# The end of the first token block: two chunks of the second product and their copies placed ahead of the second block, routing constants given a fixed place

## The chip, the core and the metric

The kernel runs as one program on one core of a Trainium2 chip. The core has five engines that each work through their own queue in order: TensorE (PE, the matmuls; PEld is its weight load), ScalarE (ACT), VectorE (DVE), GpSimd (POOL) and SyncE (SP, which here only issues DMAs). An instruction that waits for a semaphore holds up what stands behind it on its own engine. The metric is the device time of one execution in microseconds (us); lower is better.

## The reference, cut to what matters

Three stages follow one another: an attention with a band of 16 positions and 24 block summaries for each of 2 batches and 8 heads, a feed-forward layer, and a routed layer of 8 experts of which each token takes one.

```python
x = attention(q, k, v)                       # 1536 tokens x 512
h = x @ w_in                                 # 512 -> 2048
g = np.where(h > 0.0, h, np.exp(np.minimum(h, 0.0)) - 1.0)
x = g @ w_out                                # 2048 -> 512
logits = x @ w_gate
e_idx = np.argmax(logits, axis=1)            # one expert for each token
gate_w = softmax(logits)[e_idx]
eom = 1.0 / (1.0 + np.exp(-(x @ w_output_gate)))
for e in range(8):
    out[mask_e] = gate_w * eom * (np.maximum(x[mask_e] @ w1[e], 0.0) @ w2[e])
```

## The kernel before, in words

**Tiling.** The 1536 tokens are cut into 24 units of 64 queries, and these into four blocks of 8, 4, 6 and 6 units (512, 256, 384 and 384 tokens). For each block the feed-forward layer runs over 16 chunks of 128 of the 2048 hidden columns. A chunk c of block j is made of these steps: `mm_h` (line 482: 12 matmuls, hidden values h from x and the chunk of w_in, each operand in a high and a low part), `elu` (lines 495, 502 and 508: two on ACT, two on DVE, the result elp), `g_high` and `g_low` (lines 518 on ACT and 524 on DVE: high and low part of elp), `w_high` and `w_low` (lines 175 on ACT and 179 on DVE: the same of the chunk of w_out, wsp), and `mm_y` (line 543: three matmuls for each 128 tokens, added up over the chunks in the PSUM banks y). Block 0 has four y tiles, block 1 two. After chunk 15 `out_y1` copies each y tile out (line 557 on ACT; tile 1 on DVE, line 555) and stores it to DRAM by a DMA on SP's queue (line 564).

**Banks.** The y banks are four, so block 0 fills them all, and block 1's first `mm_y` needs two of them copied out. The banks for h are two, so `mm_h` of a chunk needs line 508 of the chunk two before it to be through.

**What sets the order.** Block 0 together with the attention of its own units, the conversion of the weights and the attention of block 1 is written out by hand in the string `START`, one token for an instruction group; `start_up` plays it, and all engines keep that order up to where later work is moved in. In it Yc stands for `mm_y` of chunk c, fc, gc for `g_low` and `g_high`, ic, jc for `w_high` and `w_low`, oa and ob for the attention products of units 10 and 11, ha and la for `x_hi` and `x_lo` of that pair (lines 455 and 462: the high and low part of block 1's last x), F4 for a reduction of v (line 239). After it `part1` runs steps i = 16 to 63: `mm_h` of step i, the splits, `elu`, then `mm_y` of step i - 2. So Y of chunks 14 and 15 of block 0 lies in `part1`, behind the first and the second `mm_h` of block 1, and the copies of y behind that. There only PE's order is by hand; the other engines' order is the result of a simulated schedule, which may move an instruction ahead into the stretch of `START`.

**Mid-block work.** `vsums2` brings sums of v from DVE's result to a tile pad by four DMAs on SP (line 246), and three `v_pad` on DVE (line 255) read it. Scores of the attention units 12 and 13 (line 330 on PE, line 340 on DVE, line 353 on ACT) come in step 17. `route_consts` loads 404 columns of constants by one DMA (rc) and prepares the routing tiles from them on POOL (lines 771 to 789, twelve instructions); the routing needs them once the first logits of block 0 are made. It is written at the start of block 1, and the simulated schedule moves it to the kernel's beginning, since it waits for nothing.

Of the kernel before, what the change touches and what calls it, by code (L numbers as in the profile page):

```python
# [13 lines left out]
U32 = mybir.dt.uint32  # L14
# [8 lines left out]
E, F2 = 8, 1024  # L23
# [14 lines left out]
NF = FF // 128  # L38
# [43 lines left out]
class Prog:  # L82
# [533 lines left out]
    def part1(self):  # L616
        nc = self.nc
        self.NKV = 3
        self.gate = {}
        self.prev = None  # L620
        self.rw, self.ev, self.cond = {}, {}, {}
        self.ew, self.xg, self.xs, self.g2, self.gT = {}, {}, {}, {}, {}
        self.raw, self.cvf, self.w, self.u, self.x, self.g, self.y, self.m, self.h, self.st, self.wsp = ({} for _ in range(11))
        self.ks = [self.const.tile([128, NP, NB], F32, name=f"ks{b}") for b in range(B)]
        self.v = [self.const.tile([128, 512], F32, name=f"v{i}") for i in range(self.NKV)]
        self.fv, self.mT, self.mt, self.hl, self.y2, self.o2, self.tx, self.par = {}, {}, {}, {}, {}, {}, {}, {0: 0, 1: 1}
        self.kT, self.cv, self.te, self.nmean, self.vs = {}, {}, {}, 0, None
# [12 lines left out]
        todo = {}  # L640

        def at(hs, fn, *args):
            todo.setdefault(hs, []).append((fn, args))

        for j in range(2, NBLK):
            for n in range(UNITS[j]):
                u = U0[j] + n
                h0 = PAIRS[u - n % 2]
                if UPB <= u < UPB + self.NKV:
                    at(h0 + 7, self.v_pad, u)  # L650
                at(max(2 * NF, h0 - LQ), self.load_q, u)
# [24 lines left out]

        h0 = 2 * NF * (NBLK - 1)
        at(h0 + ER, self.route_early)
        at(h0 + EI, self.early_lists)
        for n in range(2):  # L680
            at(h0 + ER + 2, self.w_expert, n)
            at(h0 + EI, self.x_load, n)
        at(h0 + XT, self.x_all, 0)
        at(h0 + XT + 3, self.x_all, 1)
        for i in range(16):
            at(h0 + max(2 * i + 1, ER + 2), self.w_load, 0, i)
            if i < WN:
                at(h0 + max(2 * i + 6, WC + i // 2), self.w_conv, 0, i)
                at(h0 + max(2 * i + 6, WC + i // 2), self.w_load, 1, i)

        def run(hs):
            for fn, args in sorted(todo.pop(hs, []), key=lambda x: rank.get(x[0].__name__, 5)):
                name = fn.__name__
                n = URGENT.get(name, 0) if hs >= 2 * NF * (NBLK - 1) else 0
                with self.tc.high_priority(offset=n) if n else ExitStack():
                    fn(*args)

        with self.tc.manual_schedule(engines={mybir.EngineType.PE}):
            for i in range(NF, len(steps)):
# [867 lines left out]
```

## Time and profile before

| | |
|---|---|
| median of 3 runs | 527.0 us (526.36 to 528.31) |
| profiled execution, its own time | 526.98 us |
| its span (first to last instruction) | 525.2 us |
| PE busy | 511.6 us, 97% of the span |
| DVE busy | 337.1 us, 64% |
| ACT busy | 305.1 us, 58% |
| POOL busy | 54.4 us, 10% |
| DMA | 78.08 MB, mean 149 GB/s |

The page's busy shares are means over the span. Matmuls are pipelined and their ends are modelled, so PE's pace is read from where one group starts to where the next starts, and its waits from the idle time in square brackets and the engine that ended it. "Granted clock" is the share of full speed that TensorE was given.

### The profile page before, as it was taken

How to read it: one execution, taken by the hardware profiler on the slowest of the kernel's cores; microseconds unless marked ns; L12 is line 12 of the kernel's file. 1: busy time of each engine (PE TensorE's matmuls, PEld its weight loads, DVE VectorE, ACT ScalarE, POOL GpSimd, SP SyncE). 2: the span in 40 equal slices, each digit the busy share in tenths (PEclk: the TensorE clock that was granted, in tenths of full speed). 3: DMA queues.
4: the chain of work that ended last, by engine and by line, in shares of the span. 5: the costliest groups of instructions: out<-in, count | busy, mean ns of one | idle time of the engine just before them, and what ended most of it. 6: DMA issues, size and time to landing. Idle time of an engine off the chain costs nothing. (4 is left out here: it accounts for less than half of the span.)

```text
span 525.2 us, 9833 instructions
## 1 busy us (share of the span) xinstructions
PE 511.6 (97%) x3325; PEld 409.6 (78%) x3325; DVE 337.1 (64%) x945; ACT 305.1 (58%) x715; POOL 54.4 (10%) x102
## 2 busy tenths in 40 slices
PE   9999999998999999999999999999999999999994
PEld 6486778886888889888898897987888567576883
DVE  5899999997688868676557899668321011535410
ACT  3899998994677658656546547543232223656421
POOL 3530000001000000000000000113411111100001
PEclk9999999999999999999999999999999999999998
DMA  8999334551311212200001025310689898594601
GB/s 293 405 396 331 119 118 140 179 195 50 132 32 52 81 45 78 82 0 16 2 0 62 1 75 192 96 61 1 183 319 302 297 360 317 174 344 149 203 22 43
DMA packets 37131, 78.08 MB, mean 149 GB/s; under 512 B 3951, under 2 KB 9807, under 8 KB 37072
## 3 DMA queue, kind: packets, MB, share of 16 engines
q1 hardware_dynamic: 34752, 70.02, 39.2%
q0 software_dynamic: 2320, 7.34, 4.0%
q8 instruction: 28, 0.46, 0.4%
q14 instruction: 31, 0.25, 0.2%
HBM read 100.37 MB, written 6.55 MB: 204 GB/s over the span
## 5 line engine op out<-in xcount | busy, mean ns | idle before, releaser
L482 PE MATMUL h<-xh,wi 128*128 128x384 f32 (+2 forms) x528 | 142.8, 338 | 2.5 <-DVE elp L508 1.5
L543 PE MATMUL y<-wsp,gh 128*128 128x512 f32 x368 | 117.3, 400 | 0.0
L482 PEld LDWEIGHTS h<-xh,wi 128*128 128x128 f32 x528 | 94.5, 190 | 10.7 <-DVE elp L508 2.4
L482 PE MATMUL h<-xl,wi 128*128 128x384 f32 (+2 forms) x264 | 87.9, 333 | 1.6 <-DVE xl L462 1.6
L543 PEld LDWEIGHTS y<-wsp,gh 128*128 128x128 f32 x368 | 66.8, 190 | 12.3 <-issue 0.5
L543 PE MATMUL y<-wsp,gl 128*128 128x512 f32 x184 | 72.5, 394 | 0.0
L1222 DVE TENSOR_TENSOR holdl<-S,holdh 128x512 fp32r<-128x512 f32 x22 | 15.2, 690 | 72.5 <-ACT holdh L1218 53.7
L1190 PE MATMUL h<-w2s,holdh 128*128 128x512 f32 x176 | 59.8, 400 | 0.0
L1233 PE MATMUL y<-w2s,holdh 128*128 128x512 f32 x176 | 59.0, 398 | 0.0
L482 PEld LDWEIGHTS h<-xl,wi 128*128 128x128 f32 x264 | 50.2, 190 | 5.6 <-DVE xl L462 1.8
L502 DVE SCALAR_TENSOR_TENSOR elt<-ele,elt 128x384 f32<-128x384 f32 (+2 forms) x64 | 35.5, 554 | 24.6 <-ACT ele L495 24.3
L495 ACT ACTIVATE elt<-h 128x384 f32<-128x384 f32 (+2 forms) x64 | 31.2, 487 | 31.1 <-PE h L482 30.5
L175 ACT CAST wsp<-wo 128x512 fp32r<-128x512 f32 x62 | 38.0, 617 | 16.8 <-PE y L543 16.0
L179 DVE TENSOR_TENSOR wsp<-wo,wsp 128x512 fp32r<-128x512 f32 x62 | 42.6, 689 | 6.3 <-ACT wsp L175 6.0
L518 ACT CAST gh<-elp 128x384 fp32r<-128x384 f32 (+2 forms) x62 | 31.5, 508 | 23.5 <-DVE elp L508 12.8
L524 DVE TENSOR_TENSOR gl<-elp,gh 128x384 fp32r<-128x384 f32 (+2 forms) x62 | 34.0, 549 | 12.2 <-ACT gh L518 11.9
L543 PEld LDWEIGHTS y<-wsp,gl 128*128 128x128 f32 x184 | 34.7, 188 | 8.0 <-DVE gl L524 0.3
L353 ACT ACTIVATE e<-e,nb 128x120 f32<-128x120 f32 x88 | 33.6, 385 | 10.8 <-DVE nb L340 10.8
L1233 PEld LDWEIGHTS y<-w2s,holdh 128*128 128x128 f32 x176 | 33.1, 188 | 8.4 <-issue 1.6
L1190 PEld LDWEIGHTS h<-w2s,holdh 128*128 128x128 f32 x176 | 33.1, 188 | 8.2 <-ACT w2s L1258 0.8
L1264 DVE TENSOR_TENSOR w2s<-wo,w2s 128x512 fp32r<-128x512 f32 x48 | 30.8, 687 | 9.3 <-ACT w2s L1258 7.8
L508 DVE SCALAR_TENSOR_TENSOR elp<-elt,h 128x384 f32<-128x384 f32 (+2 forms) x64 | 35.1, 548 | 0.9
(290 smaller groups left out, 819.8 us busy)
## 6 DMA issues: line engine op xcount, KB each, us to landing
wo<-in_w SPq DMA_DIRECT2D x9, 2048.0 KB
wo<-in_w SPq DMA_DIRECT2D x18, 1024.0 KB
ri<-in_w_in SPq DMA_DIRECT2D x16, 512.0 KB
ro<-in_w_out SPq DMA_DIRECT2D x16, 512.0 KB
wo<-in_w SPq DMA_DIRECT2D x32, 256.0 KB
w2p<-in_w SPq DMA_DIRECT2D x32, 256.0 KB
w2q<-in_w SPq DMA_DIRECT2D x24, 256.0 KB
k<-in_kw SPq DMA_DIRECT2D x18, 192.0 KB
```

The source lines that it names most:

```text
L175: self.nc.scalar.copy(w[:, 0], self.w[c, 1].bitcast(F32))
L179: self.nc.vector.tensor_tensor(w[:, 1], self.w[c, 1].bitcast(F32), w[:, 0].bitcast(F32), op=ALU.subtract)
L353: nc.scalar.activation(e[:, p], e[:, p], AF.Exp, bias=nb[:, p:p + 1], scale=-1.0, accum_out=sm[:, p:p + 1])
L482: nc.tensor.matmul(h, lhsT=w[:, wl, k * 128:k * 128 + 128], rhs=x[:, k, a:b], start=(n == 0), stop=(n == 11))
L495: self.nc.scalar.activation(self.te[j, c][i], self.h[j, c], AF.Exp if i else AF.Tanh, scale=1.0 if i else 0.5)
L502: nc.vector.scalar_tensor_tensor(t, e, 1.0, t, op0=ALU.add, op1=ALU.mult)
L508: nc.vector.scalar_tensor_tensor(p, t, 0.0, h, op0=ALU.min, op1=ALU.max)
L518: self.nc.scalar.copy(gh, p)
L524: self.nc.vector.tensor_tensor(gl, p, gh.bitcast(F32), op=ALU.subtract)
L543: nc.tensor.matmul(self.y[j][t], lhsT=gx[:, sl], rhs=wx, start=(c == 0 and n == 0), stop=(c == NF - 1 and n == len(ops) - 1))
L1190: nc.tensor.matmul(self.h[s, hf], lhsT=x[:, k], rhs=w, start=(n == 0), stop=(n == 11))
L1233: nc.tensor.matmul(self.y2[s], lhsT=g[:, ks], rhs=w, start=(i == 0 and n == 0), stop=(i == 7 and n == 2))
```

## The change

Three edits. In `START`, `X` (the routing constants) stands between `g4` and `Y3`; `Ye` and `Yf` (Y of chunks 14 and 15 of block 0) are put near the end, the second behind `ff`; and `O0` to `O3` (copy of a y tile and its store) close it. `part1` no longer plans the routing constants, and makes `mm_y` of step i - 2 only from step 18 on.

```diff
-START = "... i5 U51 C70 g4 Y3 D7 R8 ... Vf2 fe je jf gf ha F4 ff la"
+START = "... i5 U51 C70 g4 X Y3 D7 R8 ... Vf2 fe je jf gf ha Ye F4 ff Yf la O0 O1 O2 O3"
@@ part1
-        at(2 * NF, self.route_consts)
@@ part1, loop over i from NF
                 self.elu(j, c)
                 run(2 * i + 1)
-                jj, cc = steps[i - 2]
-                self.mm_y(jj, cc)
-                if cc == NF - 1:
-                    self.out_y(jj)
+                if i >= NF + 2:
+                    jj, cc = steps[i - 2]
+                    self.mm_y(jj, cc)
+                    if cc == NF - 1:
+                        self.out_y(jj)
@@ start_up
+                elif k == "X":
+                    self.route_consts()
+                elif k == "O":
+                    self.out_y1(0, *n)
```

PE at the end of block 0, before. Line 449 is the attention product ob, line 482 the first `mm_h` of block 1 (xh1, xl1: its x); Y of chunk 14 follows behind its 12 matmuls:

```order
L449 MATMUL S_1676<-et_1685,v2_100 64x64 [waits DMAHW3_49,Activation_49]
L449 MATMUL S_1676<-et_1685,v2_100 64x64 x7
L482 MATMUL h_1775<-xh1_167,wi0_545 128x256 [waits Activation_49]
L482 MATMUL h_1775<-xl1_168,wi0_545 128x256 [waits DVE_49]
L482 MATMUL h_1775<-xh1_167,wi0_545 128x256 x2
```

PE after. Behind ob stand the 12 matmuls of chunk 14 (line 543, not shown), then chunk 15 (wsp_1685, gh_1748, gl_1764), then block 1:

```order
L543 MATMUL y_822<-wsp_1685,gh_1748 128x512 [waits Activation_49]
L543 MATMUL y_822<-wsp_1685,gh_1748 128x512 [waits DVE_49]
L482 MATMUL h_1811<-xh1_167,wi0_545 128x256 [waits Activation_49]
L543 MATMUL y_822<-wsp_1685,gl_1764 128x512 [waits DVE_49]
L543 MATMUL y_823<-wsp_1685,gh_1748 128x512 x2
L543 MATMUL y_823<-wsp_1685,gl_1764 128x512
L543 MATMUL y_824<-wsp_1685,gh_1748 128x512 x2
L543 MATMUL y_824<-wsp_1685,gl_1764 128x512
L543 MATMUL y_825<-wsp_1685,gh_1748 128x512 x2
L543 MATMUL y_825<-wsp_1685,gl_1764 128x512
L482 MATMUL h_1811<-xl1_168,wi0_545 128x256 [waits DVE_49]
L482 MATMUL h_1811<-xh1_167,wi0_545 128x256 x2
```

The 24 matmuls of chunks 14 and 15 moved ahead of block 1's first `mm_h`; one matmul of that `mm_h`, which needs only xh1, came to stand inside chunk 15. Behind it the two `mm_h`, the scores and the third `mm_h` of block 1 now follow without a Y between them.

ACT behind ha (line 455), before: the two ACT steps of block 1's first `elu` (h_1775) come next, and the first copy of y stands eight rows further on:

```order
L455 CAST xh1_167<-S_1676 128x4x128 [waits PE_49]
L495 ACTIVATE elt_1791<-h_1775 128x256 [waits PE_49]
L495 ACTIVATE ele_1792<-h_1775 128x256 [waits Activation_49]
L518 CAST gh_1826<-elp_1796 128x256 [waits DVE_49,PE_49,Activation_49]
L175 CAST wsp_1913<-wo_101 128x512 [waits PE_49,Activation_49]
L495 ACTIVATE elt_1830<-h_1810 128x256 [waits PE_49]
```

ACT after:

```order
L455 CAST xh1_167<-S_1703 128x4x128 [waits PE_49]
L175 CAST wsp_1913<-wo_101 128x512 [waits DVE_49,PE_49]
L557 ACTIVATE m_1779<-y_822 128x512 [waits PE_49]
L557 ACTIVATE m_1785<-y_824 128x512 [waits PE_49]
L557 ACTIVATE m_1788<-y_825 128x512 [waits PE_49]
L175 CAST wsp_1967<-wo_101 128x512 [waits DVE_49]
L495 ACTIVATE elt_1827<-h_1811 128x256 [waits PE_49]
L495 ACTIVATE ele_1828<-h_1811 128x256
```

Three copies of y and two splits of w_out moved ahead of that first `elu`. On DVE the fourth copy and two splits (line 179) join the three `v_pad` that stood ahead of it already. On SP the four stores moved ahead of the loads of two attention units (k and q); the four pad DMAs keep their place ahead of both.

POOL in the start-up, before (rr and e: sums and exponentials of the attention of units 3, 4 and 6; cv_t: a weight chunk):

```order
L385 TENSOR_SCALAR rr_387<-sm_344 128x4 [waits Activation_49]
L771 CAST wg3_1743<-rc_1741 128x4x16 [waits DMAHW2_49]
L777 CAST tri_1750<-rc_1741 128x128
L783 COPY val_1757<-rc_1741 128x12
L784 COPY val_1757<-rc_1741 128x12
L774 TENSOR_TENSOR r_wg0_1745<-rc_1741,wg3_1743 128x64 [waits Pool_49]
L771 CAST wg3_1743<-r_wg0_1745 128x4x16 [waits Pool_49]
L385 TENSOR_SCALAR rr_429<-sm_398 128x4 [waits DVE_49]
L385 TENSOR_SCALAR rr_467<-sm_391 128x4
L774 TENSOR_TENSOR r_wg0_1745<-r_wg0_1745,wg3_1743 128x64 [waits Pool_49]
L771 CAST wg3_1743<-r_wg0_1745 128x4x16 [waits Pool_49]
L401 TENSOR_TENSOR e_350<-e_350,rr_429 128x480 [waits DVE_49,Activation_49]
```

POOL after, the same place:

```order
L385 TENSOR_SCALAR rr_387<-sm_344 128x4 [waits Activation_49]
L385 TENSOR_SCALAR rr_429<-sm_398 128x4 [waits DVE_49]
L385 TENSOR_SCALAR rr_467<-sm_391 128x4
L401 TENSOR_TENSOR e_350<-e_350,rr_429 128x480 [waits DVE_49,Activation_49]
L156 TENSOR_TENSOR cv_t_393<-cv_t_393,cv_r_394 128x512 [waits Activation_49]
```

The eight constant instructions left this stretch (and four memsets the kernel's very beginning); all twelve now stand on POOL behind its fourth copy of ks, and their DMA stands on SP behind the tenth chunk load of w_out, some 57 us into the span of before.

## Rows read from the trace of the kernel before

**Rows 1.** The page's part 1: busy us, share of span, instructions
```profile
PE 511.6 (97%) x3325; PEld 409.6 (78%) x3325; DVE 337.1 (64%) x945; ACT 305.1 (58%) x715; POOL 54.4 (10%) x102
```

**Rows 2.** Waits of PE: who, line, waited for, us, times, longest
```profile
PE h L482 <- DVE xl L462: 1.6, 1, 1.6
```

**Rows 3.** Stretches: length, busy PE PEld DVE ACT POOL, granted clock, DMA share, GB/s
```profile
42.00:125.00 83.00, 83.00 (x423) 64.81 (x421) 80.90 (x179) 75.84 (x156) 1.32 (x2) 1.00 0.52 167
126.00:129.00 3.00, 0.53 (x2) 0.33 (x3) 2.80 (x5) 0.81 (x2) 0.00 (x0) 1.00 0.25 74
129.00:133.00 4.00, 4.00 (x17) 3.62 (x18) 1.93 (x5) 0.66 (x2) 0.00 (x0) 0.57 0.02 6
```

**Rows 4.** Timeline of PE at the block's end: start, us, what, [idle before <- releaser]
```profile
125.30 0.69 PE L449 MATMUL S<-et,v 120*64 120x64 f32 x16
...
126.86 0.38 PE L482 MATMUL h<-xh,wi 128*128 128x256 f32 x1 [0.87 <-ACT xh L455]
128.85 0.39 PE L482 MATMUL h<-xl,wi 128*128 128x256 f32 x1 [1.61 <-DVE xl L462]
...
131.08 1.05 PE L543 MATMUL y<-wsp,gh 128*128 128x512 f32 x2
...
134.56 0.28 PE L482 MATMUL h<-xh,wi 128*128 128x256 f32 x1
...
136.08 0.31 PE L330 MATMUL S<-k,q 64*64 64x120 f32 x1
...
137.06 0.73 PE L543 MATMUL y<-wsp,gh 128*128 128x512 f32 x2
...
139.91 0.28 PE L482 MATMUL h<-xh,wi 128*128 128x256 f32 x1
```

**Rows 5.** Timelines of DVE and ACT there: what chunks 14 and 15 need
```profile
124.51 1.29 DVE L179 TENSOR_TENSOR wsp<-wo,wsp 128x512 fp32r<-128x512 f32 x2
125.18 0.62 ACT L518 CAST gh<-elp 128x512 fp32r<-128x512 f32 x1 [0.61 <-PE y L543]
126.91 0.68 DVE L524 TENSOR_TENSOR gl<-elp,gh 128x512 fp32r<-128x512 f32 x1
128.12 0.68 DVE L462 TENSOR_TENSOR xl<-S,xh 128x512 fp32r<-128x512 f32 x1
```

**Rows 6.** Timelines of SP, DVE and ACT behind it: pad, first elu, copy of y
```profile
126.44 3.23 SPq L246 DMA_DIRECT2D pad<-vs  x4
...
130.92 1.08 DVE L255 TENSOR_SCALAR v<-pad 24x512 f32<-24x512 f32 x3 [2.12 <-DMA pad<-vs]
...
131.32 0.38 ACT L495 ACTIVATE elt<-h 128x256 f32<-128x256 f32 x1 [4.51 <-PE h L482]
...
132.47 0.42 DVE L508 SCALAR_TENSOR_TENSOR elp<-elt,h 128x256 f32<-128x256 f32 x1
...
139.14 0.58 ACT L557 ACTIVATE m<-y 128x512 f32<-128x512 f32 x1
```

**Rows 7.** Timelines of the start-up: DVE, POOL, ACT, PE
```profile
21.08 0.62 DVE L367 TENSOR_REDUCE sm<-e 128x4 f32<-128x480 f32 x1
...
22.34 0.34 POOL L771 CAST wg<-rc 128x64 bf16<-128x64 f32 x1 [3.54 <-DMA rc<-in_rc]
...
24.24 0.52 POOL L385 TENSOR_SCALAR rr<-sm 128x4 f32<-128x4 f32 x2
24.49 0.18 DVE L391 RECIPROCAL rr<-rr 128x4 f32<-128x4 f32 x1 [1.10 <-POOL rr L385]
...
25.72 0.39 ACT L353 ACTIVATE e<-e,nb 128x120 f32<-128x120 f32 x1 [0.53 <-DVE nb L340]
...
26.58 0.65 PE L412 MATMUL T<-c,e 128*120 128x128 f32 x4 [1.06 <-POOL e L401]
```

**Rows 8.** Timelines of POOL and DVE at once, late in block 0
```profile
119.67 1.32 POOL L305 COPY k<-ks 128x96 f32<-128x96 f32 x2 [78.27 <-DVE ks L227]
...
119.97 0.68 DVE L524 TENSOR_TENSOR gl<-elp,gh 128x512 fp32r<-128x512 f32 x1
```

More of the change, by code (lines that the diff above doesn't have):

```diff
@@ L62 @@
 CP = ((0, 0),)
-START = "Lk2 Lk0 w02 Lk3 w43 Lk1 w13 x2 w42 w11 Lc0 x0 x3 w03 w20 w12 w23 w10 w50 x1 w30 w51 w53 LQ0 LQ1 Lc1 LV4 LV1 w01 w00 LW7 w22 k5 k3 w52 k1 k2 s0 s1 w21 k4 m0 s2 w32 s5 m1 m5 k0 w33 LV0 w40 m2 LW6 w41 e0 w31 M7 e1 s3 e5 s4 LV2 Lw00 m4 M2 LV3 LQ2 Lw10 M3 M0 a0 M1 e2 r0 m3 n0 t0 c0 r1 M5 M4 b4 M6 Lwd0 k7 b3 r5 k6 n1 t1 Lw01 a2 Lw30 e4 B00 n5 e3 A00 z4 P r2 c1 A10 s6 s7 z3 n2 a3 t5 p1 p0 p2 o0 c5 Lw50 r3 t2 B10 m6 p3 a4 r4 Lw51 h0 n3 l0 c2 o1 Z2 t3 e6 m7 p4 n4 c3 C00 Lq9 a6 o2 h1 Z8 o3 h2 D0 r6 Lw20 n6 h3 t4 C10 l2 Lwe0 o5 c4 l1 e7 Lw40 l3 E0 p7 t6 h5 Lw11 Lq8 B30 k8 H0 k9 r7 n7 c6 D1 p6 o4 A20 Lwf0 B20 t7 c7 o6 E1 h4 o7 C20 A30 Lw21 l5 l4 h6 h7 l6 Lw60 l7 B01 Lwa0 H1 D2 C30 G0 G1 A01 E2 C01 Lva Lw80 D3 U01 p8 Lv9 U02 E3 V01 V02 A11 B21 A21 B11 Ls00 C11 s8 C21 s9 U11 B51 B40 U12 Lqb i2 V11 A40 m8 A51 Lv8 V12 kb C40 G2 U21 Y0 Lw70 K00 Lqa D4 m9 U22 Lw31 C51 A50 B50 V21 Lwc0 A60 E4 G3 e8 V22 Y1 C50 A31 g2 j2 D5 B60 B31 C60 f2 Lw41 C31 U31 D6 E5 U32 B41 V31 ka Lw61 Ls11 E6 V32 i3 B70 A41 G4 C41 A70 K11 j3 U41 g3 U42 Y2 Lw71 G5 e9 A80 B80 V41 f3 V42 i5 U51 C70 g4 Y3 D7 R8 C80 n9 B61 Ls20 Lw90 D8 E7 E8 U52 Lwb0 V51 n8 G6 t8 A61 V52 Ba0 Aa0 U61 t9 C61 Ls01 i4 Ca0 U62 g5 c8 f4 Da G7 K20 V61 A90 j4 K01 i6 V62 c9 j5 B90 j6 f5 o8 Y4 B71 U71 Lw81 U72 A71 g6 o9 C90 Ea Ab0 V71 f6 Bb0 C71 Cb0 B81 Y5 Ls31 G8 D9 A81 V72 Db h8 E9 g7 U81 C81 Lw91 i7 l8 Eb K31 Y6 j7 Lu0 Ad0 U82 Bd0 f7 i8 B91 G9 V81 Cd0 A91 V82 j8 F0 Lu1 C91 U91 Y7 U92 sa g8 Lu5 V91 Lwa1 Lwb1 Bc0 V92 Ac0 ma F1 Dd f8 Ga F5 sb Y8 g9 Gb Cc0 Ba1 Ls30 ea Ua1 i9 Ua2 mb Va1 Aa1 eb f9 j9 K30 Ed Ra Va2 Ab1 Dc Bb1 Ub1 Ca1 Cb1 Ub2 ga Ec Lwc1 Y9 Ae0 Lu7 ia Lu2 Be0 Vb1 Gc na Vb2 Ce0 Ac1 Uc1 F7 ja Uc2 Ls21 De gb Bc1 Gd fa Cc1 Af0 ib Vc1 Bf0 F2 Vc2 ic Ee K21 Ud1 Lwd1 Ud2 Ad1 Lvb fb Ya jb Ge Lwf1 ta Yb Cf0 Bd1 Df Vd1 Ls10 Cd1 Vd2 jc Ef gc Lwe1 Af1 Bf1 Gf fc Ue1 nb Yc tb ca Ue2 gd id Lu6 Cf1 Ve1 F6 Ve2 if Lu4 K10 jd Lu3 fd Ae1 Uf1 Uf2 oa cb ge F3 Be1 Vf1 Yd Ce1 ie ob Vf2 fe je jf gf ha F4 ff la"
@@ new lines @@
+START = "Lk2 Lk0 w02 Lk3 w43 Lk1 w13 x2 w42 w11 Lc0 x0 x3 w03 w20 w12 w23 w10 w50 x1 w30 w51 w53 LQ0 LQ1 Lc1 LV4 LV1 w01 w00 LW7 w22 k5 k3 w52 k1 k2 s0 s1 w21 k4 m0 s2 w32 s5 m1 m5 k0 w33 LV0 w40 m2 LW6 w41 e0 w31 M7 e1 s3 e5 s4 LV2 Lw00 m4 M2 LV3 LQ2 Lw10 M3 M0 a0 M1 e2 r0 m3 n0 t0 c0 r1 M5 M4 b4 M6 Lwd0 k7 b3 r5 k6 n1 t1 Lw01 a2 Lw30 e4 B00 n5 e3 A00 z4 P r2 c1 A10 s6 s7 z3 n2 a3 t5 p1 p0 p2 o0 c5 Lw50 r3 t2 B10 m6 p3 a4 r4 Lw51 h0 n3 l0 c2 o1 Z2 t3 e6 m7 p4 n4 c3 C00 Lq9 a6 o2 h1 Z8 o3 h2 D0 r6 Lw20 n6 h3 t4 C10 l2 Lwe0 o5 c4 l1 e7 Lw40 l3 E0 p7 t6 h5 Lw11 Lq8 B30 k8 H0 k9 r7 n7 c6 D1 p6 o4 A20 Lwf0 B20 t7 c7 o6 E1 h4 o7 C20 A30 Lw21 l5 l4 h6 h7 l6 Lw60 l7 B01 Lwa0 H1 D2 C30 G0 G1 A01 E2 C01 Lva Lw80 D3 U01 p8 Lv9 U02 E3 V01 V02 A11 B21 A21 B11 Ls00 C11 s8 C21 s9 U11 B51 B40 U12 Lqb i2 V11 A40 m8 A51 Lv8 V12 kb C40 G2 U21 Y0 Lw70 K00 Lqa D4 m9 U22 Lw31 C51 A50 B50 V21 Lwc0 A60 E4 G3 e8 V22 Y1 C50 A31 g2 j2 D5 B60 B31 C60 f2 Lw41 C31 U31 D6 E5 U32 B41 V31 ka Lw61 Ls11 E6 V32 i3 B70 A41 G4 C41 A70 K11 j3 U41 g3 U42 Y2 Lw71 G5 e9 A80 B80 V41 f3 V42 i5 U51 C70 g4 X Y3 D7 R8 C80 n9 B61 Ls20 Lw90 D8 E7 E8 U52 Lwb0 V51 n8 G6 t8 A61 V52 Ba0 Aa0 U61 t9 C61 Ls01 i4 Ca0 U62 g5 c8 f4 Da G7 K20 V61 A90 j4 K01 i6 V62 c9 j5 B90 j6 f5 o8 Y4 B71 U71 Lw81 U72 A71 g6 o9 C90 Ea Ab0 V71 f6 Bb0 C71 Cb0 B81 Y5 Ls31 G8 D9 A81 V72 Db h8 E9 g7 U81 C81 Lw91 i7 l8 Eb K31 Y6 j7 Lu0 Ad0 U82 Bd0 f7 i8 B91 G9 V81 Cd0 A91 V82 j8 F0 Lu1 C91 U91 Y7 U92 sa g8 Lu5 V91 Lwa1 Lwb1 Bc0 V92 Ac0 ma F1 Dd f8 Ga F5 sb Y8 g9 Gb Cc0 Ba1 Ls30 ea Ua1 i9 Ua2 mb Va1 Aa1 eb f9 j9 K30 Ed Ra Va2 Ab1 Dc Bb1 Ub1 Ca1 Cb1 Ub2 ga Ec Lwc1 Y9 Ae0 Lu7 ia Lu2 Be0 Vb1 Gc na Vb2 Ce0 Ac1 Uc1 F7 ja Uc2 Ls21 De gb Bc1 Gd fa Cc1 Af0 ib Vc1 Bf0 F2 Vc2 ic Ee K21 Ud1 Lwd1 Ud2 Ad1 Lvb fb Ya jb Ge Lwf1 ta Yb Cf0 Bd1 Df Vd1 Ls10 Cd1 Vd2 jc Ef gc Lwe1 Af1 Bf1 Gf fc Ue1 nb Yc tb ca Ue2 gd id Lu6 Cf1 Ve1 F6 Ve2 if Lu4 K10 jd Lu3 fd Ae1 Uf1 Uf2 oa cb ge F3 Be1 Vf1 Yd Ce1 ie ob Vf2 fe je jf gf ha Ye F4 ff Yf la O0 O1 O2 O3"
```

## The prediction, as put on record

> **What bounds the kernel now.** I read the page's busy times first: PE is busy 97% of the span, every other engine 64% or less [rows 1]. Whatever shortens the kernel must therefore take time out of PE's line. Next the waits of PE, to see where its few pauses lie: the longest is 1.6 us before line 482, ended by xl on DVE [rows 2]. Then the stretches around it. From 42 to 125 us PE is busy in all 83.00 us, and DVE in 80.90 of them, so DVE is nearly as full as PE there [rows 3]. From 126 to 129 us PE works 0.53 us of 3; from 129 to 133 us it is busy throughout, but at a granted clock of 0.57, that is for most of it at 1.2 instead of 2.4 GHz, after the pause [rows 3]. PE's timeline tells what the pause is: the product ob starts at 125.30 and lasts 0.69 us, then the first `mm_h` of block 1 waits 0.87 us for xh on ACT and 1.61 us for xl on DVE [rows 4]. Y of chunks 14 and 15, whose inputs come earlier, stands behind it and waits in line. The second place is the start-up, where a transpose on PE waits 1.06 us for POOL [rows 7].
>
> **The boundary: what moves and what it costs.** No work is added or removed; 24 matmuls, four copies and four stores change place.
>
> Before, from the end of ob to the third `mm_h` of block 1 PE takes from 125.30 + 0.69 = 125.99 to 139.91, that is 13.92 us [rows 4]. What it does in that time, priced at full clock from the rows behind the slow stretch: one Y, 137.06 to 139.91, 2.85 us; one `mm_h`, 134.56 to 136.08, 1.52 us; the scores, 136.08 to 137.06, 0.98 us [rows 4]. Two Y, two `mm_h` and the scores make 5.70 + 3.04 + 0.98 = 9.72 us. The difference, **4.20 us**, is the pause and the slow clock; counted from the other side it is 3.00 - 0.53 = 2.47 us idle and 0.43 x 4.00 = 1.72 us of lost clock, 4.19 us together [rows 3].
>
> It goes only if the new order starves nobody. Ye would start at 125.99. Its w_out parts end by 124.51 + 1.29 = 125.80 [rows 5]; its g is older than that. Yf starts at 125.99 + 2.85 = 128.84; its high part ends at 125.18 + 0.62 = 125.80, its low part, needed third, at 126.91 + 0.68 = 127.59 [rows 5]. The matmul of block 1 that stands inside Yf needs only xh, there by 126.86 [rows 4]. Then `mm_h` at about 131.7 needs xl, through at 128.12 + 0.68 = 128.80 [rows 5]. So each input that PE waited for is 1 to 3 us early. With no pause I expect no slow clock behind it.
>
> What is late next: the third `mm_h`, at 125.99 + 9.72 = 135.71, needs one of the two h banks, so line 508 of block 1's first chunk. That chain took from 131.32 to 132.47 + 0.42 = 132.89, 1.57 us [rows 6]; the first `mm_h` now ends at 125.99 + 5.70 + 1.52 = 133.21, so the bank is free at 134.8, 0.9 us early. Ahead of it on ACT now stand three copies of 0.58 us [rows 6] and two splits. The copies can run as the y tiles finish between about 129.7 and 131.8, and the second split, which needs Yf to be through, behind the last of them, so ACT is free at about 133.0. On DVE stand the fourth copy and two splits besides the three `v_pad`, which in the trace wait for the pad DMA until 130.92 and take 1.08 us [rows 6]; issued at 126.44 on SP, ahead of the stores, that DMA has no reason to come later. DVE's copy fits in front of it. These reserves are thin: 0 to 0.9 us. The stores on SP now stand ahead of the k and q loads of two units; they can go at about 132, and I give them no cost.
>
> So the boundary gives 4.20 us. Below that: new waits of up to 0.9 us each at the third `mm_h` and at the transposes of units 12 and 13, since their scores move up by only about 2 us while the `mm_h` in front of the transposes move up by 4.2 us. Above: nothing, there is no more pause there to take.
>
> **The start-up.** DVE's sums end at 21.08 + 0.62 = 21.70, but POOL's rr comes at 24.24, since the constants, whose DMA came at 22.34, stand ahead of it [rows 7]. DVE's reciprocal loses 1.10 us by that, ACT's next exponential 0.53 us and PE's transpose 1.06 us [rows 7]. Without the constants rr can be ready before 22.4, so DVE's wait goes entirely. What is late next is the chain of exponentials on ACT, which gains its 0.53 us there and more at the PE results that it waits for behind. How much of it reaches PE is not shown by any row: at most 1.06 us, at least nothing, if another engine is just as late. From 42 us on PE has no pause at all [rows 3], so what is won before stays won provided that DVE, with 83.00 - 80.90 = 2.10 us idle there, keeps up; its own line moves up as well. I take **0.9 us**, near the upper end, because the POOL wait stands directly in front of PE and of DVE. One load fewer in the full DMA queue of the start-up is a small gain that I do not count.
>
> **The constants' new place.** Twelve POOL instructions and one DMA go to about 58 us. POOL is idle for 78.27 us up to 119.67 [rows 8], the DMA share of that stretch is 0.52 [rows 3], and the first use of the constants lies in block 1. Cost nothing, unless POOL slows DVE, which has only 2.10 us to give. The one row that shows the two at once late in block 0: two POOL copies took 1.32 us, while DVE's subtraction beside them took 0.68 us [rows 8], as it took at 126.91 without POOL [rows 5]. So POOL paid, not DVE.
>
> The Trainium skill has a rule that speaks against this place: "SBUF — State Buffer", section "Who interferes with whom", says that POOL shares a pair of ports with DVE as an exclusive lock, and that a DVE instruction with two SBUF inputs is blocked for the whole of a POOL instruction that reads SBUF if that one started first. The pair of rows just named shows the lock's other side only; by the rule the sum would lose what the third rival below loses.
>
> **Sum.** 526.98 (own time of the profiled execution, 0.02 below the median of the three) - 4.20 - 0.90 = 521.88, so **521.9 us**.
>
> **The rivals.**
> *The boundary alone.* The start-up's gain is eaten by ACT or by the DMAs before 42 us: 526.98 - 4.20 = 522.8 us. For it: DVE and ACT are nearly full from then on. Against: all of them stood behind the same POOL wait.
> *A new wait behind the boundary.* The third `mm_h` or the transposes of units 12 and 13 wait 1 us or so, because ACT carries three copies and two splits ahead of the first `elu`, and the clock falls after it as it did at 129 us. Two pauses of 0.9 us and half of the 1.72 us of clock cost 2.7 us: 521.9 + 2.7 = 524.6 us. For it: reserves of under 1 us. Against: from 129 to 133 us DVE is busy for only 1.93 and ACT for 0.66 of 4.00 us [rows 3].
> *POOL blocks DVE near 58 us.* The six constant instructions in front of rr took 24.24 - 22.34 = 1.90 us [rows 7], so the eight that read SBUF about 2.5 us; if DVE stands still for all of it, it runs 2.5 - 2.1 = 0.4 us late and PE with it, 522.3 us, or 2.5 us if DVE cannot use its idle time: 524.4 us. The rule named above is this mechanism; so far the trace bears it out on POOL's side alone.
> *Slower.* The three `v_pad` stand on DVE ahead of block 1's first `elu`, and wait for pad. If its landing is put off, by the traffic of four stores or by SP, DVE holds both h banks and PE stops. The point: the bank is needed at 135.71; `v_pad` 1.08, a split 0.69, line 502 and 508 0.9 us make 2.7 us, so pad may land until about 133.0, 2 us later than now. Each us beyond it costs PE one; slower than before by 0.5% needs 133.0 + 5.1 + 2.6 = 140.7, 10 us later than in the trace, which nothing in it announces. About 530 us.
> *The change does not do what it says:* PE's order shows that it does.
>
> **How the numbers follow.** Forecast 521.9 us: 0.55. Boundary alone, 522.8: 0.22. New wait, 524.6: 0.13. POOL blocks DVE, 522.3 to 524.4: 0.06. Slower: 0.04. About 0.5%, or 2.6 us, is what a measurement of this kernel can tell from no change, so "faster" is below 524.4. The first two, POOL and a share (0.03) of the new wait lie below: 0.86; the rest of the new wait 0.10; slower 0.04. The range of 8 in 10: down to 526.98 - 4.20 - 1.06 less the 0.6 us by which the fastest run lies under the median, 521.1, rounded to 520.9; up over the boundary alone and most of the POOL case to 524.0.
>
> **What would show it.** Right: in the profile after, PE has no pause between ob and the third `mm_h` of block 1, the granted clock is full through the boundary, and the third `mm_h` starts 5 us earlier, 4.2 of it after the end of ob; the transpose of the start-up waits for POOL no more, and the first `mm_h` of block 0 starts about 0.9 us earlier. Wrong: an idle time in front of line 482 ended by line 508, in front of line 412 ended by line 401, or a stretch of reduced clock; line 255 waiting for pad beyond 133 us; DVE durations grown near 58 us. If PE's gains show at 140 us but not in the end time, something behind has a time of its own, which I have not seen.

## The result, and the profile after

The changed kernel takes **521.6 us** (median of 6 executions, 520.85 to 524.27) against 527.4 us before in the same comparison. The ratio is 0.9899, with a 95% interval of 0.9874 to 0.9923: 5.3 us faster, 4.0 to 6.6. The forecast was 521.9 us and faster, and both came. One of its two terms did not go as told, though: the start-up's gain came, and in the profiled execution it was gone again before the boundary. This execution took 522.60 us, 4.38 less than the one of before.

The page's part 1 of the kernel after (busy us, share of the span, instructions):

```profile
PE 509.3 (98%) x3325; PEld 407.8 (78%) x3325; DVE 336.8 (65%) x945; ACT 305.5 (59%) x715; POOL 58.8 (11%) x102
```

Three stretches of it (length, busy PE PEld DVE ACT POOL, granted clock, DMA share, GB/s):

```profile
42.00:125.00 83.00, 82.58 (x419) 63.81 (x417) 80.51 (x177) 74.85 (x154) 7.63 (x14) 1.00 0.52 168
126.00:129.00 3.00, 3.00 (x14) 2.47 (x15) 2.70 (x5) 0.84 (x3) 0.00 (x0) 1.00 0.25 74
129.00:133.00 4.00, 4.00 (x25) 3.54 (x24) 2.44 (x6) 2.86 (x5) 0.00 (x0) 1.00 0.45 161
```

Against [rows 3]: the pause (PE 0.53 of 3 us) and the slow clock (0.57) behind ob are gone. But PE, which was busy in all 83.00 us from 42 to 125, now lacks 0.42 of them.

**The boundary.** PE's timeline of the kernel after, as in [rows 4]:

```profile
125.27 0.69 PE L449 MATMUL S<-et,v 120*64 120x64 f32 x16
125.89 0.73 PE L543 MATMUL y<-wsp,gh 128*128 128x512 f32 x2
...
129.19 0.28 PE L482 MATMUL h<-xh,wi 128*128 128x256 f32 x1
...
131.60 0.28 PE L482 MATMUL h<-xl,wi 128*128 128x256 f32 x1
...
134.44 0.31 PE L330 MATMUL S<-k,q 64*64 64x120 f32 x1
...
135.42 0.39 PE L482 MATMUL h<-xh,wi 128*128 128x256 f32 x1
```

From the end of ob, 125.96, to the third `mm_h`, 135.42, PE takes 9.46 us without a pause; before it was 13.92. Ob itself starts at 125.27, where it stood at 125.30. What follows on DVE, as in [rows 6]:

```profile
130.44 0.69 DVE L555 TENSOR_SCALAR m<-y 128x512 f32<-128x512 f32 x1
131.04 1.07 DVE L255 TENSOR_SCALAR v<-pad 24x512 f32<-24x512 f32 x3
...
134.27 0.42 DVE L508 SCALAR_TENSOR_TENSOR elp<-elt,h 128x256 f32<-128x256 f32 x1
```

And on ACT, behind the copies of y:

```profile
133.11 0.39 ACT L495 ACTIVATE elt<-h 128x256 f32<-128x256 f32 x1 [0.21 <-PE h L482]
```

Line 255 no longer waits for pad, ACT is free when the first h is ready, and the h bank is free at 134.69, 0.73 us ahead of its use. No new wait took the place of the old one.

**The start-up.** POOL's timeline of the kernel after, as in [rows 7]:

```profile
21.81 2.29 POOL L385 TENSOR_SCALAR rr<-sm 128x4 f32<-128x4 f32 x2 [2.76 <-DVE sm L367]
```

PE's timeline there:

```profile
25.58 0.61 PE L412 MATMUL T<-c,e 128*120 128x128 f32 x4
...
30.19 0.36 PE L482 MATMUL h<-xh,wi 128*128 128x256 f32 x1
```

POOL takes rr up as soon as DVE's sums end. The transpose on PE waits no more and comes 1.00 us earlier, the first `mm_h` of block 0 1.04 us earlier (31.23 before). So 1.04 us stand on PE at 30 us and 0.03 us at ob. One row of PE's waits is new (who, line, waited for; us, times, longest), and DVE's waits from 42 to 125 us, before and after, say where to look.

PE, kernel after:

```profile
PE h L482 <- DVE wi L167: 0.4, 1, 0.4
```

DVE, kernel before:

```profile
DVE cv_t L149 <- DMA ro<-in_w_out: 0.9, 1, 0.9
DVE vs L239 <- DMA vn<-in_vn: 0.5, 1, 0.5
DVE ks L227 <- DMA kst<-in_kT: 0.3, 1, 0.3
```

DVE, kernel after:

```profile
DVE ks L227 <- DMA kst<-in_kT: 2.0, 2, 1.8
```

DVE is gapless in long stretches, and where it pauses it waits for loads: 1.7 of its 2.10 idle us before. The load behind the long wait of the kernel after, at its issue on SP:

```profile
93.17 0.38 SPq L222 DMA_DIRECT2D kst<-in_kT  x1
```

The reduction on DVE that waits for it, and the next instruction:

```profile
97.66 0.56 DVE L227 TENSOR_REDUCE ks<-kst 128x12 f32<-128x384 f32 x1 [1.84 <-DMA kst<-in_kT]
98.13 0.68 DVE L167 SCALAR_TENSOR_TENSOR wi<-cv_t,wi 128x512 fp32r<-128x512 f32 x1
```

What that does to PE, four us later:

```profile
101.88 0.74 PE L482 MATMUL h<-xh,wi 128*128 128x512 f32 x2 [0.39 <-DVE wi L167]
```

Before, the same load was issued later, at 93.92, and was there earlier:

```profile
93.92 0.38 SPq L222 DMA_DIRECT2D kst<-in_kT  x1
...
97.14 0.55 DVE L227 TENSOR_REDUCE ks<-kst 128x12 f32<-128x384 f32 x1 [0.30 <-DMA kst<-in_kT]
```

From issue to the reduction it took 4.5 us after and 3.2 us before. DVE, 1.04 us ahead of its old line at 95 us, is 0.52 us behind it from then to 121 us, and w_in's next chunk comes late to PE. This gave **theory 1**: DVE is paced by the landing of loads, and how much of the start-up's gain reaches ob hangs on them. **Theory 2**, a rival of the prediction: POOL's constants slow DVE. They do run beside it. On POOL:

```profile
62.67 0.58 POOL L775 CAST wg<-r_wg 128x64 bf16<-128x64 f32 x1
63.20 0.72 POOL L781 CAST tri<-rc 128x128 bf16<-128x128 f32 x1
...
64.79 0.68 POOL L788 COPY val<-rc 128x12 f32<-128x12 f32 x1
```

On DVE at that time:

```profile
62.40 0.75 DVE L156 CUSTOM_DVE_ANT_0 cv_t<-cv_t,cv_r 128x1024 uint16<-128x1024 uint16 x1
63.08 0.69 DVE L401 TENSOR_TENSOR e<-e,r 128x480 f32<-128x480 f32 x1
63.69 0.51 DVE L149 TENSOR_SCALAR cv_t<-ro 128x512 int32<-128x512 int32 x1
```

Between the start of line 508 at 60.79 and of line 167 at 64.12 DVE needs 3.33 us; before it was 2.98 (61.30 to 64.28).

### The profile page after: what moved, and what is told of

Read it like the earlier page. It is cut to its first block, busy times and chain, and to the rows that moved or that the text cites. A ratio compares the mean times of both kernels' runs of the same rounds, so it can differ in the third digit from the quotient of the medians.

```text
span 520.7 us, 9835 instructions
## 1 busy us (share of the span) xinstructions
PE 509.3 (98%) x3325; PEld 407.8 (78%) x3325; DVE 336.8 (65%) x945; ACT 305.5 (59%) x715; POOL 58.8 (11%) x102
```

## The experiments

The runs that follow are read at three places on PE: the first `mm_h` of block 0; from there to ob; from the end of ob to the third `mm_h` of block 1. All us, from the profiled executions:

| kernel | first mm_h | to ob | ob's end to third mm_h | profiled time | median (executions) |
|---|---|---|---|---|---|
| before | 31.23 | 94.07 | 13.92 | 526.98 | 527.4 (6) |
| before, again | 31.50 | 94.08 | 15.12 | 528.72 | 528.3 (8) |
| before, pause filled | 31.40 | 94.09 | 12.63 | 525.31 | 525.8 (7) |
| constants alone | 30.29 | 94.09 | 12.42 | 524.01 | 526.5 (12) |
| boundary alone | 32.01 | 94.22 | 9.47 | 523.24 | 524.5 (9) |
| boundary alone, again | 30.86 | 94.08 | 9.46 | 522.87 | 524.4 (6) |
| boundary alone, start-up filled | 31.54 | 94.09 | 9.46 | 522.17 | 524.4 (7) |
| after | 30.19 | 95.08 | 9.46 | 522.60 | 521.6 (6) |
| after, again | 30.05 | 95.65 | 9.46 | 521.98 | 521.8 (6) |
| reduction later | 30.34 | 94.08 | 9.46 | 521.55 | 521.7 (6) |
| constants behind | 30.27 | 94.09 | 9.46 | 522.80 | 522.5 (5) |
| both moves | 30.12 | 94.07 | 9.46 | 521.26 | 522.5 (6) |
| wide between | 30.00 | 94.08 | 9.47 | 521.26 | 522.4 (6) |
| one product | 30.21 | 94.32 | 9.57 | 523.45 | 521.8 (6) |

**The changed kernel again** (no edit).

> The changed kernel once more, for a second profile and more rounds. The boundary: no pause on PE between ob and the third mm_h of block 1, as in the first profile. The open point is the start-up's 1.0 us, which stood on PE at 40 us (40.47 against 41.48) and was gone at ob (125.27 against 125.30). Theory 1, DVE is paced by DMA landings: the reduction of line 227 that waited 1.84 us at 97.66 waits for another length here, and ob stands where that puts it, anywhere from 124.3 to 125.3. Theory 2, POOL's constants at 61 to 65 us eat it by slowing DVE: 0.36 us lost there again and ob at 124.6 or later in every execution, however the DMA lands. End time 4.4 to 5.5 us under the kernel before.

Median 521.8 us, ratio 0.9888 (0.9857 to 0.9919), 5.9 us under 528.5. The reduction waited again, for a load issued at 93.55, and a second one earlier:

```profile
46.38 0.55 DVE L227 TENSOR_REDUCE ks<-kst 128x12 f32<-128x384 f32 x1 [0.84 <-DMA kst<-in_kT]
...
98.09 0.55 DVE L227 TENSOR_REDUCE ks<-kst 128x12 f32<-128x384 f32 x1 [1.87 <-DMA kst<-in_kT]
```

This time PE also waits at 67.12 us, 0.56 us for DVE's line 401, and ob starts at 125.70, outside the bounds that I gave theory 1. The same program lost 1.6 us on the way to ob where the first profile lost 1.0.

**Boundary alone, constants alone.** The first is the changed kernel without X and with the constants back in `part1`, the second the kernel before with X.

```diff
- C70 g4 X Y3
+ C70 g4 Y3
...
+        at(2 * NF, self.route_consts)
```

```diff
- C70 g4 Y3
+ C70 g4 X Y3
...
-        at(2 * NF, self.route_consts)
```

> The boundary's new order alone; the routing constants stay where the kernel before has them. ob at 125.3 as before, no pause behind it: third mm_h of block 1 at 135.4, 4.46 us earlier than before. End time 527.0 - 4.5 = 522.5 us. The start-up as before: a transpose on PE waits 1.06 us for POOL. If the constants' place were worth 0.9 us, this stands 0.9 us above the changed kernel; if the gain is always eaten before 125 us, level with it.

> The routing constants' new place alone; the boundary as in the kernel before. First mm_h of block 0 at 30.2 instead of 31.2, pause and slow clock behind ob as before (13.9 us from ob's end to the third mm_h). Theory 1: ob at 124.3 to 125.3 by how the loads land, end time 0 to 1.0 us under the kernel before, 0.4 in the middle. Theory 2: 0.36 us of the 1.0 always lost at 61 to 65 us, 0.6 at the most.

Boundary alone: ratio 0.9937 (0.9912 to 0.9962), 3.3 us under the kernel before, 1.2 us less gain than I expected; the stage takes 9.47 us as in the changed kernel. Its median stands 2.7 us above the changed kernel's of the same comparison (524.46 and 521.77), where I had 0.9 or nothing. Constants alone: 0.9977 (0.9957 to 0.9996), 1.2 us, where I had 0 to 1.0. Its profile had a surprise. It has the same pause as before, 0.87 and 1.66 us, but no slow clock behind it. Stretches from 125 us on (columns as above):

```profile
125.00:128.00 3.00, 0.47 (x5) 0.21 (x2) 2.92 (x5) 0.88 (x2) 0.00 (x0) 1.00 0.21 73
128.00:130.00 2.00, 2.00 (x14) 1.91 (x15) 0.00 (x0) 0.42 (x2) 0.00 (x0) 1.00 0.05 13
130.00:132.00 2.00, 2.00 (x11) 1.64 (x10) 1.84 (x5) 0.24 (x1) 0.00 (x0) 1.00 0.00 0
```

So its stage took 12.42 us, not 13.92. Here the start-up's gain reaches ob, 0.94 us at the first `mm_h` and 0.92 at ob: theory 1's "by how the loads land", with a wait of 0.92 us at 96.41 that DVE could carry.

**The reduction later.** The changed kernel with the reduction (token K30) behind four more DVE instructions.

```diff
- j9 K30 Ed Ra Va2 Ab1
+ j9 Ed Ra Va2 K30 Ab1
```

> The changed kernel with the reduction that waited for its load at 97.66 us put four DVE instructions (0.68, 0.17, 0.20, 0.63 us by their rows) further back; nothing else. Theory 1: its wait shrinks by 1.5 us to under 0.4 us, PE's 0.39 us wait before line 482 at 101.5 goes, ob at about 124.5 instead of 125.27, end time 0.4 to 0.8 us under the changed kernel of this chip. Theory 2: no difference beyond 0.2 us.

```profile
97.28 0.55 DVE L227 TENSOR_REDUCE ks<-kst 128x12 f32<-128x384 f32 x1
```

No wait stands before the reduction, none before line 482 at 101 us, and ob starts at 124.42 as theory 1 said: the way to ob takes 94.08 us, the value of before. The median, 521.7 us, is the changed kernel's within 0.1, so the expected 0.4 to 0.8 us do not show there. POOL still cost DVE time at 61 to 65 us in this run (line 401 0.69, line 149 0.51 us), and none of it reached ob: that speaks against theory 2 as the cause.

**The kernel before again, and its pause filled.** The first is unedited; the second puts matmuls of zeros into the pause.

```diff
+FILL = 24
...
+    def fill(self, n):
+        T = self.bank(self.psa, "T")
+        for _ in range(n):
+            self.nc.tensor.matmul(T[:, :256], lhsT=self.zero[:, :128], rhs=self.zero, start=True, stop=True)
...
+                if i == NF:
+                    self.fill(FILL)
                 self.mm_h(j, c)
```

> The kernel before once more, for a second profile of its boundary: e2, with the same pause of 2.5 us behind ob, showed no slow clock after it (granted clock 1.00, ob's end to the third mm_h 12.4 us), where the first profile of the kernel before showed 0.57 for 4 us (13.92 us). Theory A, the loss of clock follows every such pause: 13.9 us again, e2 an exception. Theory B, it follows in some executions only: either value; 12.4 us here would say that the pause alone is a sure gain, 2.5 us, and the clock's 1.5 to 1.7 us one that the median holds in part.

> The kernel before with 24 filler matmuls of zeros on PE between ob and the first mm_h of block 1: 24 x 0.11 us = 2.6 us of activity in the pause of 2.47 us, nothing else. It leaves the wait (PE still cannot start xl before 128.8) but takes away the idleness. If the slow clock comes from the pause: granted clock 1.00 behind it, ob's end to the third mm_h 12.2 to 12.5 us in the profile, end time 0 to 1.7 us under the kernel before, by how often its executions lose the clock (1.0 in the middle). If it comes from elsewhere: 13.9 us as before or more, since the fillers end 0 to 0.2 us after xl is there.

Stretches of the kernel before, again:

```profile
126.00:129.00 3.00, 0.65 (x11) 0.32 (x7) 3.00 (x6) 1.09 (x3) 0.00 (x0) 0.87 0.20 70
129.00:133.00 4.00, 3.76 (x14) 3.51 (x15) 1.59 (x5) 0.66 (x2) 0.00 (x0) 0.50 0.04 9
133.00:137.00 4.00, 4.00 (x19) 3.36 (x18) 0.96 (x3) 0.93 (x2) 0.00 (x0) 0.75 0.00 0
```

Stretches with the pause filled:

```profile
125.00:128.00 3.00, 3.00 (x37) 2.38 (x36) 3.00 (x7) 1.64 (x4) 0.00 (x0) 1.00 0.18 61
128.00:132.00 4.00, 3.73 (x27) 3.24 (x25) 1.90 (x5) 0.66 (x2) 0.00 (x0) 1.00 0.06 16
```

The fillers on PE's timeline, and the wait that is left:

```profile
126.11 2.79 PE L224 MATMUL T<-z 128*128 128x256 bf16 x24
128.66 0.36 PE L488 MATMUL h<-xh,wi 128*128 128x256 f32 x1
129.30 0.38 PE L488 MATMUL h<-xl,wi 128*128 128x256 f32 x1 [0.28 <-DVE xl L468]
```

The pause of before was followed by a slow clock of 1.50 us in one execution, 2.70 in another (15.12 - 12.42), and by none in the third (constants alone). This is theory B: it follows in some executions only. The other executions of the kernel before fit it: of the 69 in these comparisons 11 have a mean granted clock of 0.997 or more, 58 have 0.989 to 0.996, though at which place they lost it only a trace could tell. With the pause filled, PE gains nothing in waiting, yet the kernel is 2.1 us faster (0.9961, 0.9945 to 0.9978, of 527.9), somewhat more than the 0 to 1.7 that I expected, and its executions lie within 1.3 us (525.31 to 526.65) where those of before spread over 4.6 (524.64 to 529.26).

**The constants behind the boundary's splits, and both moves.** X goes to 120 to 129 us; the second adds the later reduction.

```diff
- C70 g4 X Y3
+ C70 g4 Y3
...
- ff Yf la O0
+ ff Yf la X O0
```

> The changed kernel with the routing constants moved once more, from 61 us to behind the last split in front of the boundary, about 128 us, where DVE is half idle. Theory 2 (POOL beside DVE costs DVE 0.36 us at 61 to 65 us): the five DVE instructions there take 0.68, 0.16, 0.64, 0.65 and 0.42 us again instead of 0.74, 0.20, 0.75, 0.69 and 0.51; if that reaches PE, ob and the end come 0.3 us earlier than in the changed kernel. Theory 1 (DVE is paced by the load that lands at 97 us): the 0.36 us turn into waiting there, ob and the end as in the changed kernel within 0.2 us.

> The changed kernel with both small moves: the reduction four DVE instructions later and the routing constants behind the last split in front of the boundary. Theory 1 with 2: between 42 and 125 us nothing on DVE waits longer than its reserve, so the start-up's gain arrives whole: first mm_h to ob 94.1 us (95.1 and 95.7 in the two profiles of the changed kernel), ob to third mm_h 9.46 us, median 0.4 to 0.8 us under 521.8, 521.2 us. If neither matters to the median, 521.8 within 0.3.

DVE with the constants behind:

```profile
61.87 0.64 DVE L156 CUSTOM_DVE_ANT_0 cv_t<-cv_t,cv_r 128x1024 uint16<-128x1024 uint16 x1
62.42 0.65 DVE L401 TENSOR_TENSOR e<-e,r 128x480 f32<-128x480 f32 x1
62.99 0.42 DVE L149 TENSOR_SCALAR cv_t<-ro 128x512 int32<-128x512 int32 x1
```

The old durations are back, so POOL did cost DVE the 0.35 us, and without it a wait of 0.99 us for the same load at 96.47 cost PE nothing. The first `mm_h` to ob takes 94.09 us, so ob comes 0.9 and 1.3 us earlier than in the two profiles of the changed kernel, more than either theory had; that the 0.35 us alone decide it is excluded by the constants alone (94.09 us) and the later reduction (94.08 us), which both kept POOL at 61 to 65 us. In the constants' new place POOL alone paid. One of its instructions beside DVE, and the next of the same kind, when DVE begins a pause:

```profile
125.12 2.07 POOL L778 TENSOR_TENSOR r_wg<-rc,wg 128x64 f32<-128x64 f32 x1
...
127.58 0.31 POOL L778 TENSOR_TENSOR r_wg<-r_wg,wg 128x64 f32<-128x64 f32 x1
```

The DVE instructions beside the first kept their 0.67 and 0.68 us.

Both moves together bring the gain to ob whole (94.07 us), and 521.26 us in the profiled execution. The medians, 522.5 us both (0.9888 and 0.9895; for both moves I had 521.2), do not tell these kernels from the changed one: 0.8 us more, where each interval reaches about 1 us either way. As versions, neither beats it.

**One product alone in the pause.**

```diff
- ha Ye F4 ff Yf la O0 O1 O2 O3
+ ha Ye F4 ff la
...
-                if i >= NF + 2:
+                if i >= NF + 1:
```

> The changed kernel with only chunk 14's product in front of block 1's first mm_h; chunk 15's product and the copies of y stand behind the second mm_h and the scores, as in the kernel before. Chunk 14's product lasts 2.85 us and the pause was 2.47, so it should cover the pause alone: xl at 128.7 is there when it ends at 128.75. Expected: no pause over 0.1 us, clock 1.00, third mm_h and end time as in the changed kernel within 0.3 us. If chunk 15 is needed too, or the copies' later place holds the scores' banks or the third mm_h: 0.5 to 1.5 us slower than the changed kernel.

As expected: 521.8 us, ratio 0.9887 (0.9867 to 0.9906), no pause behind ob, 9.57 us to the third `mm_h`. Chunk 14's product covers the pause by itself; moving chunk 15's and the copies brought 0.1 us in the trace and nothing measurable in the time.

**Two that were meant for the executions' spread.** Wide matmuls of zeros among the narrow ones of line 610 in the kernel with both moves (wide between), and, last, the start-up's pause filled in the kernel with the boundary alone; a repeat of the boundary alone ran between them.

```diff
             nc.tensor.matmul(self.L3[:, t * 16:t * 16 + 16], lhsT=mt[:, k * 128:k * 128 + 128], rhs=self.wg[:, k], start=(k == 0), stop=(k == 3))
+            if k == 3:
+                nc.tensor.matmul(self.L3[:, 256:512], lhsT=self.zero[:, :128], rhs=self.zero, start=True, stop=True)
```

> The same with four filler matmuls of 256 columns of zeros among the narrow matmuls of line 610 (16 columns each, 2.8 us at 342 us), behind which two profiles out of eight showed a granted clock of 0.50 to 0.92 for 5 us though PE had no pause in the record. Cost 4 x 0.11 = 0.45 us in every execution. If the narrow matmuls set off the slow clock: granted clock 1.00 behind them in the profile and a narrower spread, highest time under 523.2; 0.1 to 0.5 us over the kernel without the fillers at its fast executions. If they don't: the same spread, 0.45 us higher.

The trace shows three fillers, not the four that I expected. Inconclusive: the clock was full in the profile, but it was so without the fillers too; the spread stayed (521.26 to 523.79 against 521.26 to 524.13), two of the six executions still have a mean clock of 0.995, and the highest missed the 523.2.

> The boundary's new order alone, once more, to narrow its interval (ratio 0.9912 to 0.9962). Sure part 2.96 us (ob's end to the third mm_h 12.42 us with the pause and without the slow clock, 9.46 us without the pause), plus the clock, whose median share the filled pause put at about 2.1 us (0.9961 of the kernel before): 527.9 - 5.1 = 522.8 us. At 524.5 again: the median of the kernel before loses less to the clock than the filled pause says, or the start-up of this one is slower.

Ratio 0.9939 (0.9916 to 0.9962), 524.4 us: 3.2 us, nearly the same again, so 1.6 us more than the 522.8 that sure part and clock together should give.

```diff
- o1 Z2 t3
+ o1 Zb t3
```

> The boundary's new order alone, with nine more filler matmuls of zeros in the start-up where PE waits for POOL's rr (1.24 and 0.58 us in the two profiles of the boundary alone): 9 x 0.11 = 1.0 us of activity in the pause, the wait itself stays. Its median was 524.4 us twice, its profiled executions 523.2 and 522.9; the profiled ones of the changed kernel 522.6 and 522.0, median 521.7. If the start-up's pause costs its executions clock, as the boundary's does, filling it brings 0.5 to 2 us: 522.5 to 523.9 us. If they are slower because the wait itself is longer in them (the constants' load lands later), nothing changes: 524.4 within 0.5.

```profile
25.33 1.38 PE L218 MATMUL h<-z 128*128 128x256 bf16 x11
26.89 0.65 PE L412 MATMUL T<-c,e 128*120 128x128 f32 x4 [0.18 <-POOL e L401]
```

524.4 us, 0.9937 (0.9913 to 0.9961): nothing changes that these intervals could tell, and the mean granted clock of the executions does not rise either (0.9954 against 0.9959 in the 15 without the fillers). So nothing here shows clock lost behind the start-up's pause, though an effect of under about 1.5 us would not be seen. That the constants land later in those executions fits (the wait for POOL was 1.06 us in the kernel before and 1.24 and 0.58 in the two profiles of the boundary alone), but is not shown.

## Why the prediction was right, step by step

**The boundary, 4.20 us.** Every step of it held: the pause went, the clock stayed full, no input came late, the bank came 0.73 us early where I had 0.9. The stage shrank by 4.46 us; the 0.26 more are my prices, which held changeovers to the next kind of work: the last 23 of the 24 matmuls of two `mm_h` take 2.84 us in a row, 131.60 to 134.44, and with the one at 129.19, 0.12 us, 2.96 and not 3.04; two Y take 5.59, not 5.70; and Y starts 0.07 us ahead of ob's recorded end. The third `mm_h` came 4.49 us earlier, where I had named 5, since ob itself did not move. What the step did not say is that the 4.20 were two things of a different kind. The part that every execution has is 12.42 - 9.46 = 2.96 us. The clock's part of the stage was 1.50 us in the execution that I read (I had 1.72), but 2.70 and 0 in two others, and filling the pause puts it at 2.1 us in the median (1.2 to 2.9). One profile could not tell this; the term was right by the luck of the execution.

**The start-up, 0.9 us.** At the first `mm_h` it is 1.04 us in the two first profiles, and 1.24 as a mean (31.42 over six kernels with the constants in front, 30.18 over eight without; upper end in my text 1.06). The step that failed is "what is won before stays won provided that DVE, with 2.10 us idle there, keeps up". The 2.10 us, a sum over 83 us, were not in hand where they were needed. An engine that reaches a load's landing earlier waits longer there, and the landing itself moves: of the growth from 0.30 to 1.84 us 1.0 is DVE's lead and 0.52 the later landing. Taken down DVE's line, the 1.04 us went as follows: 0.25 into a wait for a load at 45.9, 0.25 into a wait for ACT at 53.0, 0.35 into POOL's constants at 61 to 65, and, after DVE had won 0.9 back where the wait of before at 79.5 us did not recur, 1.56 at 97.66. PE lost 0.2 us at 66.7 and 0.6 at 101.9. With the reduction four instructions later PE lost none of it. How much was in hand at this load the other profiles show. Waits of 0.69 to 1.07 us for it in five of them (boundary alone three times, constants alone, constants behind) cost PE 0.15 us or nothing on the way to ob; 1.51 us (one product) cost 0.25, and 1.84 and 1.87 us in the two of the changed kernel, with what they had lost at 67 us, 1.0 and 1.6. So DVE had about 1 us in hand there. Why the load landed late is open. So in the profiled execution the rival *boundary alone* (522.8) described the outcome, 522.60, by another cause than I gave it: the gain is eaten behind 42 us, not before. That the median is the sum's all the same is partly luck. The lower end of my range, 520.9, is 0.2 us under what its own terms give (521.1).

**The other rivals.** *A new wait behind the boundary*: did not come. *POOL blocks DVE*: the two do hinder each other, and the sign that I had named, longer DVE durations, did show; the size is not what I had. It cost 0.35 us of DVE, not 2.5, and at 61 to 65 us instructions of both engines took longer: POOL's cast took 0.58 instead of 0.24, DVE's line 401 0.69 instead of 0.65 us. At 125 us POOL alone paid, 2.07 instead of 0.31 us. The Trainium skill's rule ("SBUF — State Buffer", "Who interferes with whom"), by which one of the two is blocked for the whole of the other's instruction, is not what the rows at 61 to 65 us show on DVE's side: none of its instructions grew by more than 0.11 us there, and the shortest POOL instruction that reads SBUF takes 0.24. *Slower*: pad was there before DVE asked for it.

**The sum against the median.** By stages the profiled executions add up: 526.98 - 1.50 - 1.24 - 2.96 = 521.28 us, and the three kernels with both parts whose gain reaches ob whole and whose clock stays full took 521.26, 521.26 and 521.55. One execution tells no more than about 1 us, though: what follows the third `mm_h` took from 386.1 to 387.8 us in the profiled executions whose clock was full there. The medians add up less well. Clock 2.1, pause 2.96 and start-up 1.24 make 6.3 us, less the 1.0 and 1.6 that the two profiles lost on the way to ob 4.7 to 5.3; measured were 5.3 and 5.9. But the boundary alone gave 3.2 to 3.3 us three times where 5.1 were due, and its executions lie up to 4 us above its fastest. With the 1.2 us of the constants alone that makes 4.5, which the intervals do not tell from 5.3.

What lengthens an execution shows in part in its mean granted clock. Over the 69 executions of the kernel before, the time rises by 0.53 us for each 0.001 of clock that is missing (correlation -0.82), and 0.001 of 525 us is just that. At a clock of 0.997 or 0.998 the medians, pooled over the comparisons, are 526.0 us for the kernel before (11 of 69 executions), 525.6 with the pause filled (6 of 7), 523.5 with the boundary alone (10 of 22) and 521.6 with both parts and their variants (26 of 41). So with the clock nearly full the boundary brings 2.4 us and the constants' place 1.9; the rest of the gain in the median is that more executions keep their clock. Where the other 12 executions of the boundary alone lost theirs (median 524.8 us) stays open, since its three profiled ones all kept it.

## What to carry to other kernels

Read an idle time of a nearly full engine by what ends it, and place by place: idle time that a DMA ends is no sure reserve, since whoever comes earlier waits longer there and the landing moves; here about 1 us of such waiting cost nothing, and 1.8 us did. A pause of the matmul engine has a sure price, its length, and one that differs between executions, the slow clock behind it; filling the pause with matmuls of zeros separates the two in one run. Fill such a pause with the smallest piece of ready work that covers it: here one product did what two and four copies did.

## What the runs showed of the hardware

**The clock after a pause.** After the same 2.5 us of waiting in three profiles, PE's granted clock was 1.00 throughout once, 0.57 for 4 us once, and 0.50 for 4 us and 0.75 for another 4 once, that is at 1.2 GHz for part or all of these stretches.

**A slow clock without a pause.** In two of fourteen profiles the clock fell where PE has no idle time in the record, behind 2.8 us of matmuls that are only 16 columns wide. PE's timeline of the kernel with the constants behind:

```profile
341.43 2.83 PE L610 MATMUL y<-rc,mt 128*128 128x16 f32 x24
344.11 0.48 PE L1194 MATMUL h<-w2s,holdh 128*128 128x512 f32 x1
```

Two stretches of it, columns as above:

```profile
340.00:344.00 4.00, 4.00 (x37) 3.78 (x35) 1.14 (x2) 1.66 (x3) 1.52 (x3) 1.00 0.54 198
344.00:348.00 4.00, 4.00 (x16) 2.97 (x16) 2.11 (x13) 0.43 (x2) 0.00 (x0) 0.62 0.01 3
```

That is 0.38 x 4 = 1.5 us, and 1.7 with the two us behind (0.92). The same matmuls in the other kernels were followed by 1.00. That the narrow matmuls set it off was only argued.

**The size of a loss.** Added up over stretches of 2 us, what the clock lacked of 1.00 comes to 1.70 us in each of three profiles (kernel before, constants behind, one product) and to 3.42 in the fourth that shows a slow clock (kernel before, again).

**Landing of one load.** The same 192 KB load at 93 us took from its issue to its reader between 3.2 and 4.5 us in the executions in which the reader waited for it, twice 4.5 in the same program and 3.4 to 4.0 in three others of nearly the same order.
